# Attention into a two-layer network: one half's q sum moved to GpSimd, the w_in load gated one step later, a shorter run of fillers

## The chip, the cores and the metric

The kernel runs on one core of a Trainium2 chip. A core has five engines that run their own instruction streams in order and wait for each other by semaphores: TensorE (PE, matmuls; its weight loads are listed apart as PEld), VectorE (DVE), ScalarE (ACT), GpSimd (POOL) and SyncE (SP). Transfers between device memory and on-chip memory run on sixteen DMA engines; an engine only issues them. The metric is device time in microseconds (us) of one execution, lower is better.

## The reference

Inputs are q, k and v of shape 8 x 8 x 576 x 64 (batch, heads, positions, head width), and two matrices, w_in (512 x 2048) and w_out (2048 x 512). Per batch and head there are two attentions whose results are added:

```python
q_d = q.reshape(B, H, Sd, 4, D).mean(axis=3)      # and k_d, v_d: groups of four positions
out_up = np.repeat(sm_attn(q_d, k_d, v_d), 4, axis=2)
mask = np.abs(pos[:, None] - pos[None, :]) < 4      # a band of seven positions
out_local = softmax(masked scores) @ v
x = (out_up + out_local) -> (4608, 512)
h = x @ w_in;  out = (h / (1 + exp(-1.702 h))) @ w_out
```

The coarse branch needs sums of q, k and v over groups of four positions; the local branch needs only a band of the scores.

## The kernel before

**Stages.** The 4608 rows of x are worked on in nine groups of 512 tokens (`for g in range(n_groups)`, L1018). In group g, `mm1` (L821) computes x @ w_in in sixteen chunks of 128 columns (ffc), each of four accumulating 128x512 matmuls in `hps_mm` (L803), then the activation on ACT (`silu`, L816); `mm2` (L847) multiplies with w_out. Between these matmuls the steps of the next batch's attention are put in at numbered places: `POS_0` (L914) for group 0, `POS` for the others. Batch 0 has its own attention, written out line by line at L922 to L1016, ahead of all of this.

**Halves.** Heads are handled in two halves (qd 0 and 1) of four heads. For each half `prep_1` (L308) transposes k or q on DVE; `reduce_qk` (L327) sums q or k over groups of four in one DVE instruction (L331); `pool_qk` (L336) does the same in two GpSimd additions (L343, L347), and is used for the later batches. `bars0` and `scores0` (L409, L419) put a band mask and batch 0's local scores in PSUM (L411, L423); `scores_d` (L459) computes the coarse scores from the sums (L466); `exp0` and `exp_down` (L482, L502) take the exponentials on ACT (L485, L503).

**Values.** `load_vb0` (L258) loads batch 0's v in five chunks (i = 0 to 4) of 128, the last of 120, positions, converted to bf16. `prep_vd_pe` (L372) sums v over groups of four by matmuls with a selection matrix (L388): output part 0 reads chunks 0 and 1, part 1 chunks 1, 2 and 3, part 2 chunks 3 and 4; then a cast (L396) puts it in `vd`. `av_local0` (L513) applies the local weights to the chunks (matmuls at L516), `av_down0` (L523) the coarse ones to all three parts of `vd` (L529). `normalise0` (L543) divides on DVE (L546, L547). This runs for four head pairs hp = 0 to 3; their accumulators `o[hp]` are three PSUM tiles in turn, so hp 3 reuses the tile of hp 0 and starts once that has been normalised. `turned` (L999) transposes the results back by matmuls (L567) and copies them to `xT`, and `part` (L994) starts group 0's first w_in matmuls (L806).

**The loads' order.** All loads with conversion are issued by GpSimd, in the order of the code, and move on one software queue: k and q of batch 0, the five value chunks, then a gate, then w_in in three pieces (512, 512 and 1024 columns, L282), k and q of batch 1 (L218), two of the four pieces of w_out (L291), and in group 0's code the ten half chunks of batch 1's v (`load_vb`, L247, instructions at L249), two more pieces of w_out, and batch 2. The gate at L934 is a copy of one element out of value chunk 1 on GpSimd: as the engine works in order, nothing behind it is issued before that chunk has landed. Eight semaphores (99 to 106 in the trace) go round the software loads in turn, and a load is issued only when the load eight places ahead of it has landed.

**Who reads them.** Group 0's w_in matmuls read the first piece for ffc 0 to 3, the second for 4 to 7, the third for 8 to 15. Group 0's `mm2` takes its first eight matmuls (L884) from w_out piece 0, the next eight from piece 1, matmuls 17 to 32 from the same two pieces, and 33 to 48 from piece 2. Batch 1's v is first read by `prep_vd_pe(1, ...)` at place `VDP_0` = 36 (L915, L1055), the last half chunks by its last four matmuls.

**Fillers.** `warm` (L770) and the loop at L950 are matmuls on zeros whose results nobody reads: twelve of 512 columns, five of 128, five of 392, and four of 512 (L942, L943, L950, L964).

Of the kernel before, what the change touches and what calls it, by code (L numbers as in the profile page):

```python
# [15 lines left out]
TG = 512  # L16
# [3 lines left out]
def kernel(  # L20
# [9 lines left out]
    nc = tc.nc  # L30
# [3 lines left out]
    NQ = H // 4  # L34
# [28 lines left out]
    vbs = [persist.tile([128, 5, H, 65], BF16, name=f"vb{i}") for i in range(2)]  # L63
# [4 lines left out]
    for _ in range(2):  # L68
        t = work.tile([128, 2 * (S + SD)], FP32, name="l", tag="l", bufs=2).bitcast(BF16)
# [5 lines left out]
    PM = [psum.tile([128, 512], FP32, name=f"pm{i}") for i in range(2)]  # L75
# [3 lines left out]
    def pm_tile():  # L79
        turn["m"] += 1  # L80
        return PM[turn["m"] % 2]
# [17 lines left out]
    gate = consts.tile([1, 1], BF16, name="gate")  # L99
# [13 lines left out]
    def iota_band():  # L113
        for par in range(2):
            nc.gpsimd.iota(dm[halves[par]], pattern=[[-1, 60]], base=-4 * par,
                           channel_multiplier=1, **it)
# [97 lines left out]
    def load_1(name, src, store, b, qd):  # L214
        t = ldp.tile(
            [128, 1152], BF16, name=f"{name}b{qd}", tag=f"{name}b{qd}", bufs=2
        )
        nc.gpsimd.dma_start(  # L218
            out=t,
            in_=bass.AP(  # L220
                tensor=src.tensor, offset=src[b, 4 * qd].offset,
                ap=[[1152, 128], [1, 1152]],
            ),
        )
        store[b, qd] = t

    def load_qk(b, qd):
        load_1("k", k, kf, b, qd)
        load_1("q", q, qf, b, qd)
# [51 lines left out]
    def load_w_in(c, n):  # L281
        nc.gpsimd.dma_start(  # L282
            out=w_in_bf[:, :, c : c + n],
            in_=bass.AP(
                tensor=moe_w_in.tensor, offset=moe_w_in.offset + c,
                ap=[[d_ff, 128], [128 * d_ff, n_dmc], [1, n]],
            ),
        )

    def load_w_out(c):  # L290
        nc.gpsimd.dma_start(  # L291
            out=w_out_bf[:, 4 * c : 4 * c + 4, :],
            in_=bass.AP(
                tensor=moe_w_out.tensor, offset=moe_w_out.offset + c * 512 * d_model,
                ap=[[d_model, 128], [128 * d_model, 4], [1, d_model]],
            ),
        )
# [4 lines left out]
    def new_T(name, qd):  # L302
        n = S + 8 if name == "k" else S
        return work.tile([128, n, 2], BF16, name=f"{name}T{qd}", tag=f"{name}T{qd}", bufs=1)
# [3 lines left out]
    def prep_1(name, b, qd):  # L308
        store, dst = {"k": (kf, kT), "q": (qf, qT)}[name]
        tt = kT0[qd] if name == "k" and b == 0 else new_T(name, qd)  # L310
        t32 = tt[:, 0:S, :].rearrange("p t a -> p (t a)").bitcast(FP32)
        nc.vector.transpose(  # L312
            out=t32.rearrange("p (i c) -> p c i", c=18),
            in_=store[b, qd].bitcast(FP32).rearrange("p (c d) -> p c d", c=18),
        )
        dst[b, qd] = tt
# [5 lines left out]
    def new_qdT(b, qd):  # L322
        t = work.tile([128, SD, 2], BF16, name=f"qdT{qd}", tag=f"qdT{qd}", bufs=1)
        qdT[b, qd] = t
        return t

    def reduce_qk(b, qd, name):  # L327
        t = kdT[qd][:, 0:SD, :] if name == "k" else new_qdT(b, qd)
        src = (kT if name == "k" else qT)[b, qd]
        with nc.allow_low_precision("the sum is rounded once, as the pairwise one is"):  # L330
            nc.vector.tensor_reduce(  # L331
                out=t, in_=src[:, 0:S, :].rearrange("p (j f) a -> p j a f", f=4),
                axis=mybir.AxisListType.X, op=ALU.add,
            )

    def pool_qk(b, qd, names="kq"):  # L336
        for name, src in (("k", kT), ("q", qT)):
            if name not in names:
                continue
            sv = src[b, qd][:, 0:S, :].rearrange("p (j f) a -> p j f a", f=4)  # L340
            t1 = work.tile([128, SD * 4], FP32, name="pq", tag="pq")
            t1 = t1.rearrange("p (j f a) -> p j f a", f=2, a=2)
            nc.gpsimd.tensor_tensor(  # L343
                out=t1, in0=sv[:, :, 0:2, :], in1=sv[:, :, 2:4, :], op=ALU.add
            )
            dst = kdT[qd][:, 0:SD, :] if name == "k" else new_qdT(b, qd)
            nc.gpsimd.tensor_tensor(  # L347
                out=dst, in0=t1[:, :, 0, :], in1=t1[:, :, 1, :], op=ALU.add
            )
# [19 lines left out]
    def flat(p):  # L369
        return p.rearrange("p x n -> p (x n)")  # L370

    def prep_vd_pe(b, pv, kcs=range(3), eng=None, between=None):  # L372
        vb, vd = vbs[b], vds[b]

        def heads(x, j):
            if b == 0:
                return x.rearrange("p (hp j) d -> p hp j d", j=2)[:, :, j]
            return x.rearrange("p (m u j) d -> p m u j d", m=2, u=2)[:, :, j]

        for kc, iis in ((0, (0, 1)), (1, (1, 2, 3)), (2, (3, 4))):  # L380
            if kc not in kcs:
                continue
            c0 = 256 * (kc - kcs[0])
            for i in iis:
                if between:
                    between(kc, i)
                for j in range(2):
                    nc.tensor.matmul(  # L388
                        pv[64 * j : 64 * j + 64, c0 : c0 + D * HP],
                        lhsT=psel[b][i // 4][:, PSEL_AT[i, kc] : PSEL_AT[i, kc] + 64],  # L390
                        rhs=heads(vb[:, i, :, 0:D], j),
                        start=(i == iis[0]), stop=(i == iis[-1]),
                        tile_position=(0, 64 * j),
                    )
        cp = eng.tensor_copy if eng else nc.scalar.copy
        cp(  # L396
            out=vd[:, kcs[0] : kcs[-1] + 1, :, 0:D],
            in_=pv[:, 0 : 256 * len(kcs)].rearrange(
                "p (k h d) -> p k h d", k=len(kcs), h=HP
            ),  # L400
        )
# [111 lines left out]
    def av_local0(hp, o, chunks):  # L513
        for i in chunks:
            for j in range(2):
                nc.tensor.matmul(  # L516
                    o[:, j, 65 * i : 65 * i + 65],
                    lhsT=ez[hp // 2][:, hp % 2, j, i, :],
                    rhs=vbs[0][:, i, 2 * hp + j, :],
                    start=True, stop=True,  # L520
                )
# [248 lines left out]
    def warm(n, cols=512, t=None):  # L770
        t = pm_tile() if t is None else t
        for _ in range(n):
            nc.tensor.matmul(
                t[:, 0:cols], lhsT=wz[:, 0:128], rhs=wz[:, 0:cols], start=True, stop=True
            )
# [25 lines left out]
        return first + [lambda: avx(b, (0, 1)), lambda: avx(b, (2, 3))]  # L801

    def hps_mm(g, ffc, dmc, acc):  # L803
        n = TG // 2 if g == 1 and dmc and ffc < 9 else TG
        for c in range(0, TG, n):
            nc.tensor.matmul(  # L806
                acc[:, c : c + n],
                lhsT=w_in_bf[:, dmc, ffc * 128 : (ffc + 1) * 128],
                rhs=xT[dmc][:, g * TG + c : g * TG + c + n],
                start=(dmc == 0), stop=(dmc == n_dmc - 1 and c + n == TG),  # L810
            )
# [105 lines left out]
    o, y, x = {}, {}, {}  # L917
# [13 lines left out]
    for i in range(5):  # L931
        load_vb0(i)
    iota_band()
    nc.gpsimd.tensor_copy(out=gate, in_=vbs[0][0:1, 1, 0, 0:1])  # L934
    load_w_in(0, 512)
    load_w_in(512, 512)
    load_w_in(1024, 1024)
    for qd in range(NQ):
        load_qk(1, qd)
    load_w_out(0)  # L940
    load_w_out(1)
    warm(12)  # L942
    warm(5, 128)  # L943
    make_up()
    make_psel0()
    prep_1("k", 0, 0)
    prep_1("q", 0, 0)
    bars0(1, range(4))
    bars0(4, range(4))
    for _ in range(5):  # L950
        nc.tensor.matmul(
            PM[1][:, Q0:TG], lhsT=wz[:, 0:128], rhs=wz[:, Q0:TG],
            start=False, stop=True, skip_group_check=True,
        )
    for i in (4, 0, 1, 2, 3):
        scores0(0, i)
    exp0(0)
    reduce_qk(0, 0, "k")
    prep_1("k", 0, 1)
    reduce_qk(0, 0, "q")  # L960
    prep_1("q", 0, 1)
    reduce_qk(0, 1, "k")
    reduce_qk(0, 1, "q")
    warm(4, t=PM[0])  # L964
    bars0(4, range(4))
    bars0(1, (2, 3))
    exp_down(0, scores_d(0, 0, PB[2]))
# [6 lines left out]
    for hp in range(4):  # L974
        o[hp] = PB[hp % 3]
        y[hp] = y_tiles0()
    prep_vd_pe(
        0, PM[0], (0, 1), eng=nc.vector,
        between=lambda kc, i: av_local0(0, o[0], range(3 * ((kc, i) == (1, 3)))),
    )  # L980
    prep_vd_pe(0, PM[1], (2,), eng=nc.vector)
    exp_down(1, scores_d(0, 1, PB[2]))
    nc.scalar.preload_act_table_set("silu_and_others")
    for hp in range(4):
        av_local0(hp, o[hp], range(0 if hp else 3, 5))
        av_down0(hp, o[hp])
        normalise0(o[hp], y[hp])
    make_dm()
# [29 lines left out]
    for g in range(n_groups):  # L1018
        b = g + 1
# [69 lines left out]
```

## Time and profile before

| what | value |
|---|---|
| median of three runs | 313.85 us (313.32 to 314.01) |
| the profiled execution: its own time | 312.69 us |
| its span, first to last instruction | 310.9 us |
| granted TensorE clock in it | 1.00 |
| TensorE busy | 299.7 us, 96% |
| ACT, DVE, GpSimd busy | 203.4, 148.3, 146.9 us |
| moved by the DMA engines | 39.93 MB, 128 GB/s on average |

The span leaves out 1.8 us of the execution's own time. A profile lists instructions by line, engine, operation and operands (out<-in), with the time of one and the idle time of the engine ahead of it; the chain that ended last follows the end back through whatever released each piece of work. The time from issuing a transfer to its landing stands in the list of issues.

### The profile page before, as it was taken

Reading aid. Unit: us, or ns where it says so; the run is one execution under the profiler, and the core shown is the slowest. Engines: PE = TensorE matmul, PEld = TensorE weight load, DVE = VectorE, ACT = ScalarE, POOL = GpSimd, SP = SyncE. Lnnn points to the kernel's source line nnn. Section 1 sums busy time; section 2 is a strip of 40 time slices with the busy share of each in tenths; the row PEclk is TensorE's granted clock in tenths of the full one; section 3 lists DMA queues with packets and bytes.
Section 4 is the critical chain, followed back from the end, with each engine's and each line's share of the span. In section 5 each row is a group of like instructions: output and inputs, shape, how many; then the busy total and the mean of one; then the engine's idle time right before and its main releaser. Section 6 shows DMA issues by size and latency. Waiting matters only on the chain.

```text
span 310.9 us, 9597 instructions
## 1 busy us (share of the span) xinstructions
PE 299.7 (96%) x4138; PEld 156.2 (50%) x4181; DVE 148.3 (48%) x304; ACT 203.4 (65%) x327; POOL 146.9 (47%) x169
## 2 busy tenths in 40 slices
PE   8899999999999999999999999999999999999995
PEld 3464555665544464455545554555455544444444
DVE  6984936851694159505970499038902760000000
ACT  4755766777858786768866885589558857216511
POOL 8542393394229933894369634983396110000000
PEclk9999999999999999999999999999999999999999
DMA  6999999899527942795159705981430110010011
GB/s 110 138 208 209 185 136 216 241 201 226 161 94 163 206 120 87 166 224 139 70 168 201 177 36 174 193 211 39 137 89 34 39 70 0 34 67 36 0 67 67
DMA packets 64042, 39.93 MB, mean 128 GB/s; under 512 B 44544, under 2 KB 54912, under 8 KB 64000
## 3 DMA queue, kind: packets, MB, share of 16 engines
q0 software_dynamic: 18784, 14.94, 32.9%
q1 hardware_dynamic: 45072, 24.32, 28.0%
q8 instruction: 32, 0.52, 0.7%
q14 instruction: 10, 0.08, 0.1%
q10 hardware_dynamic: 144, 0.07, 0.1%
HBM read 44.81 MB, written 9.44 MB: 174 GB/s over the span
## 4 chain that ended last, share of the span: by engine, by line
PE 91%; DMA 2%; issue 2%; POOL 2%; ACT 1%; DVE 1%; POOLq 0%; DVEq 0%; ACTq 0%
PE pm L884 36%; PE pm L806 24%; PE pa L806 16%; PE pa L439 3%; DMA vb<-in_v_dram 2%; PE pa L884 2%; PE pa L696 2%; PE pa L674 2%; PE pa L466 2%; PE pm L899 1%; POOL vb L260 1%; PE pa L609 1%; PE pa L567 1%; PE pa L597 0%; POOL kb L218 0%
## 5 line engine op out<-in xcount | busy, mean ns | idle before, releaser
L884 PE MATMUL pm<-w_out_bf,gT 128*128 128x512 bf16 x503 | 114.6, 379 | 3.4 <-issue 3.2
L806 PEld LDWEIGHTS <-w_in_bf 128*128 128x128 bf16 x603 | 58.3, 98 | 63.8 <-issue 0.3
L806 PE MATMUL pm<-xT,w_in_bf 128*128 128x512 bf16 (+1 forms) x342 | 86.9, 375 | 0.6
L884 PEld LDWEIGHTS <-gT 128*128 128x128 bf16 x560 | 52.7, 98 | 62.4 <-issue 0.6
L817 ACT ACTIVATE gT<-pm 128x512 bf16<-128x512 f32 x88 | 52.7, 603 | 41.0 <-PE pm L806 41.0
L806 PE MATMUL pa<-xT,w_in_bf 128*128 128x512 bf16 (+1 forms) x245 | 59.0, 361 | 0.3
L511 DVE TENSOR_TENSOR es<-es,mask 128x600 bf16<-128x600 bf16 x28 | 17.2, 651 | 85.6 <-ACT es L477 85.5
L869 ACT ACTIVATE osb<-pm 128x512 f32<-128x512 f32 (+2 forms) x35 | 20.3, 583 | 30.5 <-PE pm L884 25.1
L817 ACT ACTIVATE gT<-pa 128x512 bf16<-128x512 f32 x56 | 32.1, 608 | 6.3 <-PE pa L806 6.3
L766 POOL TENSOR_TENSOR xT<-xT,od 128x576 bf16<-128x576 bf16 x12 | 15.4, 1280 | 40.0 <-DVE xT L750 40.0
L750 DVE TENSOR_TENSOR xT<-n,l 128x285 bf16<-128x285 f32 (+1 forms) x96 | 28.1, 366 | 0.0
L343 POOL TENSOR_TENSOR pq<-kT 128x576 f32<-128x576 bf16 x11 | 12.8, 1160 | 30.4 <-DVE kT L312 30.4
L871 DVE TENSOR_SCALAR osb<-pm 128x128 f32<-128x128 f32 x1 | 0.3, 291 | 53.8 <-ACT osb L869 53.8
L360 POOL TENSOR_TENSOR pq<-v 112x512 f32<-112x512 f32 x18 | 23.7, 1317 | 3.9 <-DMA v<-in_v_dram 3.9
L312 DVE STREAM_TRANSPOSE kT<-kb 128x576 f32<-128x576 f32 x16 | 19.9, 1244 | 4.4 <-DMA kb<-in_k_dram 4.4
L312 DVE STREAM_TRANSPOSE qT<-qb 128x576 f32<-128x576 f32 x16 | 19.8, 1238 | 0.3
L503 ACT ACTIVATE ed<-pa 128x864 bf16<-128x864 f32 x16 | 14.3, 894 | 7.2 <-PE pa L466 7.2
L477 ACT ACTIVATE es<-pa 128x600 bf16<-128x600 f32 x28 | 17.2, 669 | 0.1
L745 ACT ACTIVATE l<-l 128x1440 f32<-128x1440 f32 x12 | 16.8, 1404 | 0.4
L740 DVE COPY n<-pa 128x492 f32<-128x492 f32 x24 | 15.0, 665 | 2.7 <-ACT l L739 2.0
L739 ACT ACTIVATE l<-pa 128x492 f32<-128x492 f32 x24 | 12.6, 578 | 4.6 <-PE pa L696 3.7
L439 PE MATMUL pa<-qT,kT 32*64 32x60 bf16 x1120 | 15.4, 195 | 0.0
(132 smaller groups left out, 355.0 us busy)
## 6 DMA issues: line engine op xcount, KB each, us to landing
out_dram<-osb SPq DMA_DIRECT2D x34, 256.0 KB, 2.2
vf<-in_v_dram SPq DMA_DIRECT2D x60, 128.0 KB, 4.9
v<-in_v_dram SPq DMA_DIRECT2D x72, 96.0 KB, 3.1
kb<-in_k_dram POOLq DMA_DIRECT2D x16, 288.0 KB, 6.5
qb<-in_q_dram POOLq DMA_DIRECT2D x16, 288.0 KB, 8.6
w_out_bf<-in_moe_w_out_dram POOLq DMA_DIRECT2D x4, 512.0 KB, 13.2
w_in_bf<-in_moe_w_in_dram POOLq DMA_DIRECT2D x2, 512.0 KB, 6.8
w_in_bf<-in_moe_w_in_dram POOLq DMA_DIRECT2D x1, 1024.0 KB, 12.2
```

What stands on the lines that cost most here:

```text
L312: nc.vector.transpose(out=t32.rearrange("p (i c) -> p c i", c=18), in_=store[b, qd].bitcast(FP32).rearrange("p (c d) -> p c d", c=18),)
L360: eng.tensor_tensor(out=t1[0:112], in0=x[:, :, 0:2, :], in1=x[:, :, 2:4, :], op=ALU.add)
L439: nc.tensor.matmul(P[1 + r // 2][64 * par : 64 * par + 64, r % 2, 60 * i : 60 * i + 60], lhsT=kT[b, qd][rows, k0 : k0 + 64, a], rhs=qT[b, ...
L477: nc.scalar.activation(out=es[2 * qd + u][:, :, 0:300], in_=sp[u][:, :, 0:300], func=AF.Exp, scale=inv_sqrt_d,)
L511: nc.vector.tensor_tensor(out=ev, in0=ev, in1=mask, op=ALU.mult)
L745: nc.scalar.activation(out=l, in_=l, func=AF.Exp, scale=-1.0)
L750: nc.vector.tensor_tensor(out=out, in0=sub(n, *part), in1=sub(l, *part), op=ALU.mult)
L766: eng.tensor_tensor(out=xs, in0=xs, in1=sub(od[:, u, :], 0, (1, SD), (0, 4)), op=ALU.add)
L806: nc.tensor.matmul(acc[:, c : c + n], lhsT=w_in_bf[:, dmc, ffc * 128 : (ffc + 1) * 128], rhs=xT[dmc][:, g * TG + c : g * TG + c + n], star ...
L817: nc.scalar.activation(out=gT[:, ffc, :], in_=acc, func=AF.Silu, scale=GELU_SCALE)
L869: eng.activation(out=osb, in_=ap, func=AF.Copy, scale=1.0 / GELU_SCALE)
L884: nc.tensor.matmul(ops[t], lhsT=gT[:, ffc, t * 128 : (t + 1) * 128], rhs=w_out_bf[:, ffc, :], start=(ffc == 0), stop=(ffc == n_ffc - 1),)
```

## The change

GpSimd now forms the coarse sums of q of half 0 of batch 0 (`pool_qk(0, 0, "q")`) in the place of DVE's `reduce_qk(0, 0, "q")`. The gate copies from value chunk 3 instead of chunk 1, and stands, with the loads behind it, after that sum in GpSimd's order. Ten filler matmuls are dropped: the five of 128 columns, one of the five at L950, and the four of L964. DVE's two sums of half 1 follow their transposes directly. On TensorE, all of part 0 and 1 of `prep_vd_pe`, then the local products of hp 0 for chunks 0 to 3, then the coarse scores of half 1 come ahead of part 2 (which needs chunk 4); after it come the rest of hp 0's local products and all of hp 1's, ahead of hp 0's coarse ones. In group 1, ffc 9 to 12 are now also computed in two half-width matmuls for three of the four accumulation steps, as ffc 0 to 8 already were: twelve more matmuls.

```diff
     def hps_mm(g, ffc, dmc, acc):
-        n = TG // 2 if g == 1 and dmc and ffc < 9 else TG
+        n = TG // 2 if g == 1 and dmc and ffc < 13 else TG
...
     iota_band()
-    nc.gpsimd.tensor_copy(out=gate, in_=vbs[0][0:1, 1, 0, 0:1])
-    load_w_in(0, 512)
...
-    warm(12)
-    warm(5, 128)
+    warm(12)
     make_up()
...
-    for _ in range(5):
+    for _ in range(4):
         nc.tensor.matmul(
...
     exp0(0)
     reduce_qk(0, 0, "k")
+    pool_qk(0, 0, "q")
+    nc.gpsimd.tensor_copy(out=gate, in_=vbs[0][0:1, 3, 0, 0:1])
+    load_w_in(0, 512)
...
     prep_1("k", 0, 1)
-    reduce_qk(0, 0, "q")
+    reduce_qk(0, 1, "k")
     prep_1("q", 0, 1)
-    reduce_qk(0, 1, "k")
     reduce_qk(0, 1, "q")
-    warm(4, t=PM[0])
...
-    prep_vd_pe(
-        0, PM[0], (0, 1), eng=nc.vector,
-        between=lambda kc, i: av_local0(0, o[0], range(3 * ((kc, i) == (1, 3)))),
-    )
-    prep_vd_pe(0, PM[1], (2,), eng=nc.vector)
+    prep_vd_pe(0, PM[0], (0, 1), eng=nc.vector)
+    av_local0(0, o[0], range(4))
     exp_down(1, scores_d(0, 1, PB[2]))
     nc.scalar.preload_act_table_set("silu_and_others")
+    prep_vd_pe(0, PM[1], (2,), eng=nc.vector)
+    av_local0(0, o[0], range(4, 5))
+    av_local0(1, o[1], range(5))
     for hp in range(4):
-        av_local0(hp, o[hp], range(0 if hp else 3, 5))
+        if hp > 1:
+            av_local0(hp, o[hp], range(5))
         av_down0(hp, o[hp])
         normalise0(o[hp], y[hp])
```

More of the change, by code (lines that the diff above doesn't have):

```diff
@@ L370, in flat, with prep_vd_pe @@
         return p.rearrange("p x n -> p (x n)")
-    def prep_vd_pe(b, pv, kcs=range(3), eng=None, between=None):
+    def prep_vd_pe(b, pv, kcs=range(3), eng=None):
         vb, vd = vbs[b], vds[b]
@@ L384, in prep_vd_pe @@
             for i in iis:
-                if between:
-                    between(kc, i)
                 for j in range(2):
@@ L933 @@
     iota_band()
-    nc.gpsimd.tensor_copy(out=gate, in_=vbs[0][0:1, 1, 0, 0:1])
-    load_w_in(0, 512)
[L936 to L941, printed above, removed]
     warm(12)
-    warm(5, 128)
     make_up()
@@ L958 @@
     reduce_qk(0, 0, "k")
+    pool_qk(0, 0, "q")
+    nc.gpsimd.tensor_copy(out=gate, in_=vbs[0][0:1, 3, 0, 0:1])
+    load_w_in(0, 512)
+    load_w_in(512, 512)
+    load_w_in(1024, 1024)
+    for qd in range(NQ):
+        load_qk(1, qd)
+    load_w_out(0)
+    load_w_out(1)
     prep_1("k", 0, 1)
-    reduce_qk(0, 0, "q")
+    reduce_qk(0, 1, "k")
     prep_1("q", 0, 1)
-    reduce_qk(0, 1, "k")
     reduce_qk(0, 1, "q")
-    warm(4, t=PM[0])
     bars0(4, range(4))
```

## The prediction

> **What bounds the kernel.** I read the page's busy shares first, then the chain that ended last in order of time, then the timelines of GpSimd and TensorE and the DMA issues around the places that the change touches.
>
> ```profile
> PE 299.7 (96%) x4138; PEld 156.2 (50%) x4181; DVE 148.3 (48%) x304; ACT 203.4 (65%) x327; POOL 146.9 (47%) x169
> ...
> PE 91%; DMA 2%; issue 2%; POOL 2%; ACT 1%; DVE 1%; POOLq 0%; DVEq 0%; ACTq 0%
> ```
>
> TensorE is busy 96% of the span and 91% of the last chain. The rest of the chain is the beginning; its pieces are start, length, what:
>
> ```profile
> 6.32 1.73 POOL vb L260 x2
> 8.05 7.71 DMA vb<-in_v_dram
> 16.11 0.51 PE pa L466 x24
> 17.53 1.10 DVE y L547
> 18.68 0.47 PE pa L516 x10
> ```
>
> So the end hangs on value chunk 4 (issued at 8.05, landed at 15.76), then on matmuls, DVE's first normalisation (17.25 to 18.62), hp 3, and TensorE without a pause worth naming. What the change can save lies ahead of 18.7 us; what it can cost lies wherever a later load is then missed. GpSimd's timeline shows the loads (start, length, what, idle before):
>
> ```profile
> 9.00 0.47 POOL L115 IOTA dm<- 64x60 f32 x2
> 12.56 0.18 POOL L934 COPY gate<-vb 1x1 bf16<-1x1 bf16 x1 [3.08 <-DMA vb<-in_v_dram]
> 12.79 2.29 POOL L282 DMA_DIRECT2D w_in_bf<-in_moe_w_in_dram  x3
> ...
> 37.77 2.10 POOL L249 DMA_DIRECT2D vb<-in_v_dram  x3 [2.15 <-DMA w_out_bf<-in_moe_w_out_dram]
> 39.86 1.52 POOL L291 DMA_DIRECT2D w_out_bf<-in_moe_w_out_dram  x2
> ```
>
> The reader should see that the last three half chunks of batch 1's v, 25 us behind the gate, still wait for the queue: they are issued 0.28 us after w_out piece 1 lands (37.49). The stretch table gives 199 to 219 GB/s from 16 to 36 us without a hole. **The software queue is saturated from the first w_in packet to about 40 us, so a later start of w_in moves every landing behind it by as much.**
>
> **DVE and GpSimd.** Gone from DVE is one sum at 10.29, 1.29 us long. But the second half's k sum (1.29 us) moves into its place, so q's transpose still ends near 12.75 and the second scores still start at 12.79; only half 1's last sum ends earlier, near 14.0 instead of 15.14. GpSimd gets two additions of 1.147 and 0.666 us (rows L343 and L347 of later batches). It is free at 9.47 and has waited until 12.56, so they end at 9.5 + 1.15 + 0.67 = 11.3, where DVE's sum ended at 11.58: the first coarse scores (11.64) gain 0 to 0.2 us and then wait for the transpose anyway. Price 0. If GpSimd were slowed by DVE beside it, its cover lasts until the gate's chunk lands, more than 3 us.
>
> **Fillers.** TensorE idles between the first and the second scores (0.30 us at 10.56, 0.57 at 12.22). Ten fillers less (five of 128 columns and one of 392, 0.2 to 0.5 us in all, and four of 512 at 8.89, 1.04 us) make it idle longer before the same data. Price 0. As for the twenty instructions (a weight load and a matmul each) by which the stream is shorter, the trace shows one 16 KB code transfer in this stretch, from 14.28 to 15.74, ending with chunk 4's last semaphore step at 15.76. Moving it could bring chunk 4 between 0 and 0.5 us earlier (the other fetches mostly take 0.9 to 1.1 instead of 1.47), and delay it as much if it collides otherwise; the next step shows why I take 0.
>
> **The order on TensorE.** Rows of before:
>
> ```profile
> 14.55 0.35 PE L516 MATMUL pa<-vb,l 128*128 128x65 bf16 x6
> 14.86 0.42 PE L388 MATMUL pm<-vb,psel 128*64 128x256 bf16 x4
> 15.81 0.30 PE L388 MATMUL pm<-vb,psel 128*64 128x256 bf16 x2 [0.53 <-DMA vb<-in_v_dram]
> 16.04 0.58 PE L466 MATMUL pa<-qdT,kdT 32*64 32x144 bf16 x24
> ```
>
> Afterwards the path starts from chunk 3, not chunk 4. Chunks 0 to 3 landed at 11.35, 12.51, 13.52, 14.82: steps of 1.16, 1.01, 1.30. Without w_in's descriptors written beside the fourth (12.79 on), I take 1.08, the mean of the first two: 14.6, with 14.5 and 14.82 as ends. From there: two matmuls of L388 (0.22), eight of L516 (0.41 by the six in 0.31), 24 of L466 (0.51), four of L388 (0.42), some 0.1 for two switches of shape: 14.64 + 1.66 = 16.3, where part 2's cast began at 16.22. Chunk 4 is there by then, even at 15.76. So TensorE's idle 0.53 us is filled, but the cast starts within -0.05 to +0.3 us of where it did, most likely +0.1. The first normalisation follows 1.03 us later as before, and hp 1's local products, now done early, leave TensorE idle in front of hp 3, which waits for that normalisation. **Expected gain at the start: none, -0.1 us.**
>
> **The gate.** It opened 0.28 us after its chunk (12.51 to 12.79). With chunk 3 at 14.6 w_in is issued at 14.88, 2.1 us later. Not all of that is lost, because w_in could not run at once:
>
> ```profile
> GB/s 152 160 155 149 152 152 157 155 155 157 157 152 152 149 138 131 122 90 73 61 45 46 210 97 87 42 10 0 0 31 20 72 123 143 164 205 195 215 205 174
> ```
>
> These are 40 slices of 12 to 16 us. The value chunks fade out by 14.3; the first w_in packet starts at 14.32, and full rate is reached at 15.3. By 16.0 some 171 packets of 1 KB had gone; at 197 per us that equals a start at full rate at 15.13. For an issue into an empty queue the nearest row is the first load of the kernel, k at 1.24: first packet 1.40 us after issue, and its bytes by 4.0 us (196 KB at 190 per us) equal full rate from 2.97, 1.73 after issue. w_in's descriptors take 0.80 us against 0.69, so 1.8: 14.88 + 1.8 = 16.68. **The queue moves by 16.68 - 15.13 = 1.55 us.** Ends: chunk 3 at 14.5 and 1.3 us to full rate (the shortest first packet of the later k loads is 1.27) give 0.95; 14.82 and 2.0 give 2.0.
>
> By the Trainium skill (DMA: Bandwidth & Descriptors, Specifications), a GpSimd-issued transfer has a first-byte latency of about 1 us; an estimate by that is a queue moved by 0.75 us. The rows here show 1.27 to 1.49 for k and 1.53 for w_in, so the trace speaks for the dearer price, and the sum does not use the page.
>
> **Who misses it.** Landing now, plus 1.55, against the reader (landing from the issue list: issue plus time to landing):
> - w_in pieces: 18.75, 21.29, 26.56, read at 20.89, 25.05, 29.37: still 0.6 us or more in time. k and q of batch 1 shift DVE's sums from 37.6 to 39.2, read at 40.31: in time.
> - w_out piece 1: 37.49 to 39.04, read by the ninth L884 matmul at 39.36: just in time.
> - batch 1's v, last half: 43.00 to 44.55; its reader is the 13th of the fourteen L388 matmuls, at 44.02. TensorE's queue took its release 0.10 us after landing, and some 0.15 goes to the start: late by 0.78.
> - w_out piece 2 (39.86 + 7.2 = 47.0) to 48.57, read by the 33rd L884 matmul at 47.83: with 0.15 late by 0.9, the first 0.78 of which is already lost.
>
> ```profile
> 43.43 0.97 PE L388 MATMUL pa<-vb,psel 128*64 128x256 bf16 x14
> 44.34 1.04 PE L884 MATMUL pa<-w_out_bf,gT 128*128 128x512 bf16 x4
> ...
> 47.83 0.38 PE L884 MATMUL pm<-w_out_bf,gT 128*128 128x512 bf16 x1
> ```
>
> Both readers have about 0.7 us to spare, so TensorE loses the shift less 0.7: 0.85 us, and any gain or loss at the start of up to that size is swallowed there. Behind it TensorE has no idle time that could give it back.
>
> **Group 1's halves.** Eight half-width matmuls run from 59.65 to 60.53, 0.110 us each, two of them 0.220 against 0.216 for a full one: twelve pairs cost 0.05 us. The shift of the later stream by two pairs I price at 0 (loops repeat in 32.35 to 32.42 us).
>
> **Sum.** 0 + 0 + 0.85 + 0.05, the start swallowed: +0.9 us on the profiled execution's 312.69 (span 310.9 and 1.8 around it). That execution is 1.16 below the median of the runs, so I add it to the median: 314.75.
>
> **Rivals.**
> - *The spare time swallows it.* If the queue moves by 0.9 to 1.3 us, the readers miss 0.2 to 0.6 us at most: 313.7 to 314.4, within 0.2% (0.63 us, about what this kernel's measurement can tell from no change). For it: the low ends above. Against it: k's slow first packets.
> - *The values come earlier, so it is faster.* One mechanism: w_in's descriptor writing is what slows the value chunks, in the slices from 13.3 on where the rate falls from 152 to 45. If chunk 3 lands at 14.2 or before, the cast starts at 15.9 and the first normalisation 0.4 us earlier or more; the gate then opens at 14.5 and with a short start the queue moves by about 0.7, which the spare time covers. At 14.0 this gives 0.65 us: 313.2. It decides from chunk 3 before 14.3. Against it: chunks 1 and 2, undisturbed, came in steps of 1.0 to 1.16, which puts chunk 3 at 14.5.
> - *TensorE loses its full rate.* The first eleven fillers start 427 ns apart, the later ones up to twice as fast, so TensorE starts at half rate. The four dropped fillers were 1.04 of 2.88 us busy from 9 to 13. If it fell back, the 3 to 5 us of matmuls behind 12.8 would cost 1.5 to 2.5 us more: 316. Against it: the 0.57 and 0.53 us pauses of before did not trigger it. The Trainium skill (TensorE: Matmul & The Clock Gate, Part 1) has the half rate return after an idle window of about 3.4 us; no pause here is that long.
> - *The edits do not reach the path* (GpSimd's sum and the code fetch, above): then the gate alone decides, as forecast.
>
> **Chances.** Forecast, later loads: 0.55, own range 314.5 to 315.6. Swallowed: 0.28. Faster: 0.12. Half rate: 0.05. Slower 0.60, same 0.28, faster 0.12. The range, 313.5 to 315.8, leaves out most of the faster case and the half rate.
>
> **What would show it.** The gate copy near 14.7 and w_in at 14.9; first w_in packet near 16.3; w_in's first piece landing at 20.3, batch 1's last values near 44.5; a pause of about 0.8 us in the L388 group at 44 or in front of the 33rd L884 matmul near 48.5; the first normalisation between 17.2 and 17.6. It is wrong if w_in's landing moves by under 1 us, or if TensorE shows no pause between 43 and 49 us.

## The result and the profile after

The changed kernel takes **316.26 us** (median of 8 runs, 315.26 to 317.43) against 313.93 us for the kernel before in the same rounds (8 runs, 313.07 to 315.44). The ratio is **1.0072**, 95% interval 1.0047 to 1.0097: slower by some 2.3 us, where 0.9 was forecast. The profiled execution took 315.53 us, with a span of 313.8 us (before: 310.9).

The page of the changed kernel: the busy times, the 40 slices of the granted clock, and the shares of the chain that ended last.

```profile
span 313.8 us, 9646 instructions
...
PE 304.2 (97%) x4183; PEld 157.3 (50%) x4183; DVE 149.6 (48%) x303; ACT 203.4 (65%) x327; POOL 150.4 (48%) x171
...
PEclk9989999999999999999999999999999999999999
...
PE 80%; DMA 12%; ACT 2%; DVE 2%; POOL 2%; issue 1%; DVEq 0%; POOLq 0%; ACTq 0%
```

Two things are new. DMA had 2% of the chain and has 12%. The clock row has an 8 in its third slice (15.7 to 23.5 us): part of it ran at less than full clock. TensorE's 4.5 us more of busy time (299.7 before) are not to be read as cost: the trace of before lacks 43 matmul records (4138, with 4181 weight loads).

The chain of the changed kernel in order of time (start, length, what; the first 62 us):

```profile
7.19 8.17 DMA vb<-in_v_dram
...
15.41 0.18 POOL gate L949
...
15.64 5.53 DMA w_in_bf<-in_moe_w_in_dram
...
21.45 19.42 DMA w_out_bf<-in_moe_w_out_dram
...
41.16 4.81 DMA vb<-in_v_dram
...
46.01 0.41 PE pa L386 x4
```

Read downwards: value chunk 3 lands at 15.36, the gate opens, w_in is issued at 15.64, w_out and the last half chunks of batch 1's v wait for their place in the queue, and TensorE's last sums of those values wait for their landings (45.97 on this chain, 46.38 for the last half chunk). Before, no load after the start was on the chain. (Lines of the changed code stand two lower: L386 here is L388 before, L882 is L884, L647 is L649.)

GpSimd's timeline in the changed kernel (start, length, what, idle before and its cause), then TensorE's:

```profile
10.79 0.67 POOL L347 TENSOR_TENSOR qdT<-pq 128x288 bf16<-128x288 f32 x1
15.41 0.18 POOL L949 COPY gate<-vb 1x1 bf16<-1x1 bf16 x1 [3.96 <-DMA vb<-in_v_dram]
15.64 2.31 POOL L282 DMA_DIRECT2D w_in_bf<-in_moe_w_in_dram  x3
...
41.16 2.03 POOL L249 DMA_DIRECT2D vb<-in_v_dram  x3 [2.43 <-DMA w_out_bf<-in_moe_w_out_dram]
43.16 1.53 POOL L291 DMA_DIRECT2D w_out_bf<-in_moe_w_out_dram  x2
```

```profile
44.30 1.02 PE L882 MATMUL pa<-w_out_bf,gT 128*128 128x512 bf16 x4
45.25 1.57 PE L386 MATMUL pa<-vb,psel 128*64 128x256 bf16 x14
46.76 1.04 PE L882 MATMUL pa<-w_out_bf,gT 128*128 128x512 bf16 x4
```

The fourteen L386 matmuls took 0.97 us before and take 1.57; the 0.6 between are two waits of some 0.3 us, for half chunks that land at 45.97 and, the last one, at 46.38 (43.00 before). At the end of this group TensorE is at 46.82, before it was at 44.40: 2.4 us late. In this execution 1.8 of them were there when the group began (45.25 against 43.43); they come from the start. At the end of the span it is 2.9 late.

The stretches from 14 to 19 us in the changed kernel; the last three columns are the granted clock, the DMA share and GB/s:

```profile
14.00:14.50 0.50, 0.50 (x11) 0.40 (x12) 0.42 (x1) 0.50 (x1) 0.00 (x0) 1.00 2.90 72
15.00:15.50 0.50, 0.10 (x2) 0.10 (x1) 0.00 (x0) 0.50 (x2) 0.09 (x1) 0.83 0.06 1
16.50:17.00 0.50, 0.50 (x24) 0.47 (x16) 0.13 (x1) 0.00 (x0) 0.50 (x1) 0.50 0.00 0
17.50:18.00 0.50, 0.50 (x9) 0.26 (x6) 0.08 (x1) 0.50 (x1) 0.50 (x2) 0.50 0.63 53
18.50:19.00 0.50, 0.50 (x26) 0.49 (x24) 0.00 (x0) 0.50 (x1) 0.50 (x2) 0.75 1.20 199
```

From 15 to 17 us hardly a byte moves, and full rate returns at some 18.2 (15.3 before). And the clock is at half from 15.33 to 18.75 us.

### The profile page after: what moved, and what is told of

The parts are those of the page before. It is cut to its first block, busy times and chain, and to the rows that moved or that the text cites. A ratio compares the mean times of both kernels' runs of the same rounds, so it can differ in the third digit from the quotient of the medians.

```text
span 313.8 us, 9646 instructions
## 1 busy us (share of the span) xinstructions
PE 304.2 (97%) x4183; PEld 157.3 (50%) x4183; DVE 149.6 (48%) x303; ACT 203.4 (65%) x327; POOL 150.4 (48%) x171
## 4 chain that ended last, share of the span: by engine, by line
PE 80%; DMA 12%; ACT 2%; DVE 2%; POOL 2%; issue 1%; DVEq 0%; POOLq 0%; ACTq 0%
PE pm L882 35%; PE pm L804 22%; PE pa L804 13%; DMA w_out_bf<-in_moe_w_out_dram 6%; DMA vb<-in_v_dram 4%; PE pa L437 3%; PE pa L694 2%; PE pa L672 2%; DMA w_in_bf<-in_moe_w_in_dram 2%; PE pa L464 1%; PE pm L897 1%; ACT l L640 1%; DVE xT L647 1%; ACT l L629 1%; POOL vb L260 1%
## 5 line engine op out<-in xcount | busy, mean ns | idle before, releaser
L882 PE MATMUL pm<-w_out_bf,gT 128*128 128x512 bf16 x528 | 119.4, 379 | 0.0
L804 PEld LDWEIGHTS <-w_in_bf 128*128 128x128 bf16 x615 | 59.5, 98 | 63.1 <-issue 0.7
L804 PE MATMUL pm<-xT,w_in_bf 128*128 128x512 bf16 (+1 forms) x370 | 89.0, 369 | 0.3 <-ACT osb L867 0.2
L882 PEld LDWEIGHTS <-gT 128*128 128x128 bf16 x560 | 52.8, 98 | 62.3 <-issue 0.4
L509 DVE TENSOR_TENSOR es<-es,mask 128x600 bf16<-128x600 bf16 x28 | 18.7, 707 | 82.7 <-ACT es L475 82.6
L764 POOL TENSOR_TENSOR xT<-xT,od 128x576 bf16<-128x576 bf16 x12 | 16.7, 1394 | 38.1 <-DVE xT L748 37.8
L437 PE MATMUL pa<-qT,kT 32*64 32x60 bf16 x1120 | 15.4, 195 | 0.0
```

Of the source, the lines that this page charges most:

```text
L437: nc.tensor.matmul(P[1 + r // 2][64 * par : 64 * par + 64, r % 2, 60 * i : 60 * i + 60], lhsT=kT[b, qd][rows, k0 : k0 + 64, a], rhs=qT[b, ...
L509: nc.vector.tensor_tensor(out=ev, in0=ev, in1=mask, op=ALU.mult)
L764: eng.tensor_tensor(out=xs, in0=xs, in1=sub(od[:, u, :], 0, (1, SD), (0, 4)), op=ALU.add)
L804: nc.tensor.matmul(acc[:, c : c + n], lhsT=w_in_bf[:, dmc, ffc * 128 : (ffc + 1) * 128], rhs=xT[dmc][:, g * TG + c : g * TG + c + n], star ...
L882: nc.tensor.matmul(ops[t], lhsT=gT[:, ffc, t * 128 : (t + 1) * 128], rhs=w_out_bf[:, ffc, :], start=(ffc == 0), stop=(ffc == n_ffc - 1),)
```

## The experiments

The main theory was that the gate alone (chunk 3 instead of 1, two chunks later) makes the loss, through the queue. Rivals: the new order on TensorE and the half clock at the start; the dropped fillers; GpSimd's sum. The half-width chunks of group 1, priced 0.05 us, were not run alone. The ratios are against the kernel before, run on the same chip in turn; its medians there lie between 313.09 and 314.07.

| run | ratio [95%] | w_in issued | batch 1's v all landed | first normalisation | first activation of group 1 |
|---|---|---|---|---|---|
| before | 1 | 12.79 | 43.00 | 17.25 | 61.60 |
| after | 1.0072 [1.0047, 1.0097] | 15.64 | 46.38 | 19.07 | 64.30 |
| e1: after, gate 1 | 1.0033 [1.0014, 1.0052] | 13.04 | 43.80 | 17.67 | 62.09 |
| e2: before, gate 3 | 1.0099 [1.0075, 1.0123] | 15.39 | 46.08 | 17.23 | 63.80 |
| e3: after, fillers back | 1.0112 [1.0078, 1.0145] | 16.48 | 46.99 | 18.75 | 65.61 |
| e4: before, new order | 1.0034 [1.0015, 1.0054] | 13.24 | 43.98 | 19.32 | 63.68 |
| e8: before, fewer fillers | 1.0010 [0.9995, 1.0025] | 13.05 | 43.17 | 17.40 | 62.30 |
| e12: before, GpSimd's sum | 0.9999 [0.9978, 1.0021] | 12.94 | 43.98 | 17.48 | 62.40 |

The last four columns are from one profiled execution each; chunk 3's landing alone lies between 14.7 and 16.2 us in the profiled executions of all kernels.

### One part undone, one part alone: e1 to e4

e1 is the changed kernel with the gate back, e2 the kernel before with the gate moved:

```diff
e1   -    nc.gpsimd.tensor_copy(out=gate, in_=vbs[0][0:1, 3, 0, 0:1])
e1   +    nc.gpsimd.tensor_copy(out=gate, in_=vbs[0][0:1, 1, 0, 0:1])
e2   -    nc.gpsimd.tensor_copy(out=gate, in_=vbs[0][0:1, 1, 0, 0:1])
e2   +    nc.gpsimd.tensor_copy(out=gate, in_=vbs[0][0:1, 3, 0, 0:1])
```

> The changed kernel with the gate back on value chunk 1; everything else stays changed. Queue theory (the loss is w_in's later issue, carried by the full software queue to batch 1's v at 45 us): w_in is issued near 12.8 to 13.2 us, batch 1's last value half lands near 43.0 to 43.5, and the loss of 2.3 us shrinks to what is left of the start, 0 to 0.7 us. Start theory (the loss is the new matmul order and TensorE's half rate before 19 us): the first normalisation stays near 18 to 19 us and the kernel stays 1.5 us or more slower than before.

> The kernel before with the gate on value chunk 3 and nothing else. Queue theory: w_in is issued 2.3 to 2.9 us later, batch 1's last value half lands that much later (45.3 to 45.9), the time rises by that less some 0.6 us: 1.7 to 2.3 us slower. Start theory: within 0.3 us of before.

Measured: 1.0033 and 1.0099. The gate alone costs 3.1 us, all that the whole change costs and more (1.7 to 2.3 were expected); with the gate back, 1.0 us stays, somewhat above the 0.7 allowed for. TensorE of e2:

```profile
37.59 1.90 PE L884 MATMUL pm<-w_out_bf,gT 128*128 128x512 bf16 x8
40.48 1.02 PE L884 MATMUL pm<-w_out_bf,gT 128*128 128x512 bf16 x4 [0.99 <-DMA w_out_bf<-in_moe_w_out_dram]
...
44.75 0.91 PE L388 MATMUL pa<-vb,psel 128*64 128x256 bf16 x12
46.21 0.30 PE L388 MATMUL pa<-vb,psel 128*64 128x256 bf16 x2 [0.55 <-DMA vb<-in_v_dram]
```

The second wait is the one of the changed kernel, at the same place (there it lies inside the group), with the old order, all fillers and a full clock. The first one the changed kernel does not have: with TensorE on time, the ninth L884 matmul already waits 0.99 us for w_out piece 1, which lands at 40.44 (37.49 before). In the changed kernel's profile TensorE came 1.8 us later, and that piece (40.87) was there. **The gate is the cause of the main loss.**

e3 is the changed kernel with its ten fillers back, e4 the kernel before with the new order on TensorE:

```diff
e3   +    warm(5, 128)
e3   -    for _ in range(4):
e3   +    for _ in range(5):
e3   +    warm(4, t=PM[0])
e4   -    prep_vd_pe(0, PM[0], (0, 1), eng=nc.vector, between=...)
e4   -    prep_vd_pe(0, PM[1], (2,), eng=nc.vector)
e4   +    prep_vd_pe(0, PM[0], (0, 1), eng=nc.vector)
e4   +    av_local0(0, o[0], range(4))
     ...
e4   +    prep_vd_pe(0, PM[1], (2,), eng=nc.vector)
e4   +    av_local0(0, o[0], range(4, 5))
e4   +    av_local0(1, o[1], range(5))
     ...
```

> The changed kernel with the ten fillers put back. Queue theory: TensorE keeps its full rate and the first normalisation comes near 17.5 to 18 instead of 19.07, but batch 1's v still lands near 46, so the time stays 2.0 us or more above before. Start theory: 1 to 1.8 us of the 2.3 come back.

> The kernel before with the new order of the first value products alone (part 0 and 1, local products of hp 0 for chunks 0 to 3, coarse scores, part 2, the rest). Queue theory: the first normalisation moves by -0.1 to +0.4 us and the time by as much. Start theory, as far as it blames the order: 0.5 to 1 us slower.

Measured: 1.0112 and 1.0034. The fillers do not bring the time back; by the medians e3 is no faster than the changed kernel (316.16 against 316.26). Its first normalisation came at 18.75, not at 17.5 to 18; chunk 3 landed late in that execution (16.19). The order alone costs 0.34%, with the old gate, some 1.1 us, which is what the start theory gave; the first normalisation moves by 2.07 us, where the main theory had 0.4 at most. TensorE of e4:

```profile
15.76 0.30 PE L388 MATMUL pm<-vb,psel 128*64 128x256 bf16 x2 [1.07 <-DMA vb<-in_v_dram]
15.99 0.57 PE L516 MATMUL pa<-vb,l 128*128 128x65 bf16 x8
16.49 0.93 PE L466 MATMUL pa<-qdT,kdT 32*64 32x144 bf16 x24
```

Chunk 3 landed at 15.71 in this execution, and the local products that filled this wait before now stand behind it. From 16.10 to 19.51 the clock is at half: the 24 coarse scores take 0.93 us, as in the changed kernel, where e1 with a full clock shows 0.58:

```profile
15.32 0.42 PE L514 MATMUL pa<-vb,l 128*128 128x65 bf16 x8
15.67 0.58 PE L464 MATMUL pa<-qdT,kdT 32*64 32x144 bf16 x24
16.18 0.49 PE L386 MATMUL pm<-vb,psel 128*64 128x256 bf16 x4
```

The half clock is not there in every execution. Six of ten of e1 have a mean clock below 0.996; they take 314.78 us on average, the four others 313.50. The kernel before averages 313.26 beside them, so most of what e1 loses is the half clock. In e4 the two below take 314.96 and the four others 313.63: about half of its loss. (3.41 us at half clock take 0.005 off the mean of an execution.)

### The dose: e5, e6, e7

The kernel before with the gate on chunk 0 (e5), 2 (e6) and 4 (e7) instead of 1.

> The kernel before with the gate on value chunk 0, nothing else: w_in issued 1.1 us earlier. Queue theory: batch 1's last value half lands about 1.1 us earlier, but it was in time already, so the time stays (within 0.4 us), unless w_in now slows the value chunks, which would show as chunk 4 landing later and the first normalisation after 17.3. Start theory says nothing of it.

> The kernel before with the gate on value chunk 2: w_in issued 1.0 us later. Queue theory with the whole shift of the issue passed on and 0.7 us to spare at batch 1's v: 0.3 to 0.6 us slower. If instead a part of the shift is hidden by the value chunks' own drain, as the prediction had it: no change.

> The kernel before with the gate on value chunk 4: w_in issued 3.2 to 3.5 us later. Queue theory: 0.8 to 1.0 us slower than with chunk 3, so 3.5 to 4 us above before; the pause in front of batch 1's v grows by as much and w_out piece 1 or the first w_in piece may be missed too.

| gate on chunk | w_in issued | w_in's first step landed | batch 1's v all landed | ratio [95%] |
|---|---|---|---|---|
| 0 | 11.94 | 17.01 | 42.71 | 1.0015 [0.9987, 1.0042] |
| 1 (before) | 12.79 | 17.80 | 43.00 | 1 |
| 2 | 13.83 | 18.80 | 43.91 | 1.0033 [1.0017, 1.0050] |
| 3 (e2) | 15.39 | 20.22 | 46.08 | 1.0099 [1.0075, 1.0123] |
| 4 | 16.28 | 21.20 | 47.20 | 1.0123 [1.0099, 1.0147] |

Issue and landing move together, within 0.25 us, and the time follows from chunk 2 on. From w_in's issue to its first packet it takes 1.50 to 1.53 us with gates 1 to 4 and 1.66 with gate 0, whether chunks still drain ahead of it or the queue is empty. **Of a later issue 0.2 us at most was hidden by the values ahead of it** (e2: issued 2.60 us later, first step landed 2.42 later). An earlier one (e5) gains nothing that can be measured.

Who waits changes with the dose. e6 cost 1.0 us where 0.3 to 0.6 was expected, and in its profile TensorE waits for no late load. In e7 the pause in front of batch 1's v was expected to grow, and it is gone: TensorE loses the time earlier, to w_in's first piece, and the L388 group then takes 0.98 us. TensorE of e7:

```profile
22.88 1.03 PE L806 MATMUL pm<-xT,w_in_bf 128*128 128x512 bf16 x2 [1.59 <-DMA w_in_bf<-in_moe_w_in_dram]
...
46.66 0.98 PE L388 MATMUL pa<-vb,psel 128*64 128x256 bf16 x14
```

### Fewer fillers, and GpSimd's sum: e8, e12

e8 is the kernel before without the ten fillers. e12 is it with `pool_qk(0, 0, "q")` on GpSimd, the gate and the loads behind it, and DVE's order of the changed kernel.

> The kernel before without the ten fillers, nothing else. Queue theory: nothing moves in the queue; no change, except in executions in which TensorE falls to half rate for a window before 19 us, which cost about 1 to 1.5 us each. If the fillers hold the rate, such executions appear here and the median rises by 0.3 to 1 us; if the order's empty wait alone causes them, none appear.

> The kernel before with the first q half's sum on GpSimd (and DVE's order as in the change), nothing else; the gate stays on chunk 1. By the prediction's step: the sum ends near 11.4, the second scores still start near 12.8 to 13.1, and the time is the same within 0.3 us.

Measured: 1.0010 and 0.9999. Neither edit can be told from no change by itself. But five of the ten executions of e8 have a mean clock below 0.996, which only one of 92 of the kernel before has: without these fillers the clock is lost in part of the executions, with the old order too. It costs nothing there: the five take 313.79 us on average, the five others 313.84. The profiled execution of e8 is one with a full clock, so where its half clock lies is not shown.

### A shorter queue: e9 and its control e10

w_in's third piece is loaded with 512 columns instead of 1024, so 512 KB less lie ahead of batch 1; e9 does it in the changed kernel, e10 in the kernel before. The last 512 columns of w_in are left out, and ffc 12 to 15 compute with the weights of 8 to 11, so the product is another one while the work stays.

```diff
-                lhsT=w_in_bf[:, dmc, ffc * 128 : (ffc + 1) * 128],
+                lhsT=w_in_bf[:, dmc, (ffc - ffc // 12 * 4) * 128 : (ffc - ffc // 12 * 4 + 1) * 128],
...
-    load_w_in(1024, 1024)
+    load_w_in(1024, 512)
```

> The changed kernel, but only the first 512 of the last 1024 columns of w_in are loaded, and chunks 12 to 15 compute with the weights of 8 to 11 (so a part of the product is another one; the work of every engine stays). Gate, order and fillers stay changed. Queue theory: 512 KB less ahead of batch 1's loads give back about 2.5 us of queue, its v lands near 43.5 again, and the time falls from 2.3 to 3 us above before to 0.3 to 1.2, what the start costs. Start theory: the time stays where it was.

> The control: the same shortened w_in load in the kernel before (chunks 12 to 15 compute with the weights of 8 to 11). Queue theory: every later landing 2.5 us earlier, but nothing waited for them: within 0.3 us of before, at most 0.3 us faster where executions had batch 1's loads late.

Measured: e9 1.0018 [0.9992, 1.0044], e10 0.9981 [0.9960, 1.0002]. In e9 w_in is issued as late as in the changed kernel (15.52), yet batch 1's v has landed at 43.96 and the group has no wait:

```profile
45.69 0.97 PE L386 MATMUL pa<-vb,psel 128*64 128x256 bf16 x14
```

So the late issue does no harm by itself; it costs because the queue has no slack up to batch 1's values. In e9 the half clock shows again: five executions below 0.996 take 314.86 us on average, the five above 313.41. (The profiled one has it, so its group starts late; but 43.96 would be in time for the kernel before too, and w_out piece 1 landed at 38.83.)

### A second place, GpSimd's wait for w_out: e11, e13, e14

The trace shows a second reader that the late queue delays, one that the prediction did not look at. GpSimd waits in its order for w_out's piece 3 (the gate of batch 2's values), and only then adds `od` to `xT`. Before, this addition ended (50.91) just ahead of DVE's next product; in the changed kernel it runs beside it. GpSimd, then DVE, of the changed kernel:

```profile
52.53 0.17 POOL L918 CAST vf<-w_out_bf 1x1 f32<-1x1 bf16 x1 [2.81 <-DMA w_out_bf<-in_moe_w_out_dram]
52.68 1.20 POOL L658 TENSOR_TENSOR xT<-xT,od 128x576 bf16<-128x576 bf16 x1
```

```profile
50.35 0.31 DVE L647 TENSOR_TENSOR od<-n,l 128x144 f32<-128x144 f32 x1 [0.55 <-ACT l L640]
53.46 0.59 DVE L647 TENSOR_TENSOR od<-n,l 128x144 f32<-128x144 f32 x1 [0.81 <-ACT l L640]
```

The same product takes 0.31 us alone and 0.59 beside the addition. This is not peculiar to a late queue: in the profiles of e8 and e12, with w_in as early as before and no loss that can be told, it takes 0.84 and 0.88; in that of e6 0.89. To test it, the gate of batch 2's values is moved to piece 2, in the kernel before (e11), in the changed kernel (e13) and in e1 (e14):

```diff
-            load_v(2, gate=after(w_out_bf[0:1, 12, 0:1], nc.gpsimd))
+            load_v(2, gate=after(w_out_bf[0:1, 8, 0:1], nc.gpsimd))
```

> The kernel before with batch 2's first value load held back by w_out's piece 2 instead of piece 3, so that GpSimd is free for its additions of x some 2.5 us earlier (near 47 instead of 49.6). If the second place of loss is GpSimd's addition running beside DVE's product at 51 us, this product takes 0.31 us in every execution and the time is the same or up to 0.5 us less than before; if that place does not matter, or the earlier value load disturbs w_out's last piece, the same or slower.

> The changed kernel with one wait of GpSimd's moved: batch 2's values are issued once w_out's piece 2 has landed instead of piece 3, so GpSimd no longer stands at L918 until 52.5 us and its xT addition (1.20 us) can end before DVE's product od at 53.5 us. Theory A, the late queue costs in two places (batch 1's last values in front of TensorE, then GpSimd's wait for w_out): od takes 0.31 us again instead of 0.59, and the ratio falls from 1.0072 by 0.1 to 0.2 points, to 1.0052 to 1.0062. Theory B, only the wait for batch 1's values costs: od is 0.31 us all the same, but the ratio stays at 1.0072 within its interval, since another wait ends last. Theory C, the loads issued earlier push other loads back: the ratio rises above 1.0085.

> The changed kernel with the gate of w_in back at value chunk 1 (1.0033 by itself) and the same move of GpSimd's wait to w_out's piece 2. Theory A, part of those 0.33% comes from GpSimd's wait and DVE's product beside its addition: 1.0015 to 1.0025. Theory B, the 0.33% come from the start alone (values' order on TensorE, its half rate from about 15 us in part of the executions): 1.0033 within its interval.

Measured: e11 0.9991 [0.9969, 1.0012], e13 1.0081 [1.0053, 1.0110], e14 1.0010 [0.9991, 1.0030]. In e13 the product is back at 0.31 us and group 1's first activation comes at 64.04 instead of 64.30. But the time is no better than the changed kernel's. DVE, GpSimd and TensorE of e13 show where the 0.26 us went:

```profile
53.47 0.31 DVE L647 TENSOR_TENSOR od<-n,l 128x144 f32<-128x144 f32 x1 [0.81 <-ACT l L640]
```

```profile
78.55 1.41 POOL L360 TENSOR_TENSOR pq<-v 112x512 f32<-112x512 f32 x1 [5.25 <-DMA vf<-in_v_dram]
```

```profile
82.84 0.26 PE L672 MATMUL pa<-ed,vd 48*64 48x144 bf16 x4 [0.46 <-POOL vd L363]
```

Batch 2's values, now issued from 50.47 on, before w_out's last piece has landed (52.87), come later at their end: their second copies need 7.8 us from issue to landing (median) instead of 6.1. GpSimd starts summing them at 78.55 instead of 77.92, and TensorE waits 0.46 us for that sum, where it did not wait in the changed kernel. The expectation that the ratio falls by 0.1 to 0.2 points failed, though its step (the product at 0.31) came true. For e14 the ratio is 0.23 points under e1's, but the intervals overlap; it isn't settled. Its executions split as e1's do: seven below 0.996 take 314.87 us, the five others 313.93.

No version tried is clearly faster than the kernel before.

## Why the prediction was right in its direction and wrong in its size

**The chain was right.** Later gate, later queue, batch 1's last half chunk late, TensorE waits in the L388 group, nothing gives it back. The gate alone (e2) does that, the profile of the changed kernel has the pause at the place named (0.6 us instead of 0.8, with TensorE already 1.8 us late), and the shortened queue (e9) removes it.

**The step that failed is the size: "The queue moves by 16.68 - 15.13 = 1.55 us."** Measured: w_in's issue moved by 2.85 us, the first step of its landing by 2.83 (17.80 to 20.63), batch 1's last landing by 3.38. The 1.28 us between 1.55 and 2.83 are two errors.
- *"Not all of that is lost, because w_in could not run at once"* took 0.55 us off. I had read the slow start of w_in as a wait for the value chunks to drain. The dose runs show 1.50 to 1.53 us to the first packet behind any gate from 1 to 4, so the delay moves with the issue. My comparison row, k's first load, is another load and reaches full rate sooner: 1.73 us after its issue by my reckoning, where w_in took 15.13 - 12.79 = 2.34.
- *Chunk 3 at 14.6* was 0.76 us early: it landed at 15.36. Of this, 0.48 was there at chunk 2 (14.00, before 13.52). Chunk 2 landed between 13.52 and 14.39 in the profiled executions of all kernels, so the single profile that I built on was the earliest of them: bad luck. The other 0.28 is the step, 1.36 instead of 1.08. I had reckoned that without w_in's descriptors beside it the fourth chunk would come in a step like the first two. Without them the step was 1.14 to 1.80 us (six profiles), with them 1.18 to 1.80 (ten), so the descriptors do not show as what slows it. It was in the trace of before that it came 1.30 behind chunk 2; I explained that away.

With 3.38 for the last half chunk the same sum gives 2.4 us, near the 2.3 measured: its matmul, the 13th of the group, starts at 44.13 before (I had 44.02), and in the changed kernel it starts 0.14 after the landing, so 44.13 - 43.00 - 0.14 = 0.99 us were to spare, and 3.38 - 0.99 = 2.39. That it fits so well is partly luck. For the gate alone the sum comes out low: 2.1 against 3.1 us (e2), nothing against 1.0 (e6), 3.2 against 3.9 (e7). What adds 0.7 to 1.0 us there is open. The rest of the shift in the queue, 3.38 against 2.83, came on the way; its cause I did not test.

**The readers.** w_in's pieces and k and q of batch 1 were in time, as forecast. w_out piece 2 was not late on TensorE, since the loss had already been taken. w_out piece 1, which the forecast had just in time, is late as soon as the queue moves by the measured amount and TensorE does not: e2 waits 0.99 us for it, the larger of its two waits. That GpSimd itself stands in front of w_out piece 3 was missing in the list; the cost of that in the changed kernel stays unproven, as e13 gave 0.26 us back and lost 0.46 elsewhere.

**DVE and GpSimd, priced 0.** GpSimd's sum ended at 11.46 (forecast 11.3). The second scores came at 13.09 instead of 12.79, so not quite free in that execution, but e12 alone shows no cost (0.9999). **Fillers, priced 0:** e8 agrees in the time (1.0010, not told from 1), but not in the clock, which falls in half of its executions.

**The order on TensorE, priced -0.1.** Wrong: e4 costs 0.34%. The first normalisation came at 19.07, 1.8 us late, not within 0.3. TensorE of the changed kernel:

```profile
13.09 0.23 PE L421 MATMUL pm<-qT,kT 32*128 32x120 bf16 x2 [1.01 <-DVE qT L312]
...
15.40 0.43 PE L386 MATMUL pm<-vb,psel 128*64 128x256 bf16 x2 [0.56 <-DMA vb<-in_v_dram]
15.76 0.62 PE L514 MATMUL pa<-vb,l 128*128 128x65 bf16 x8
16.31 0.93 PE L464 MATMUL pa<-qdT,kdT 32*64 32x144 bf16 x24
17.17 0.64 PE L386 MATMUL pm<-vb,psel 128*64 128x256 bf16 x4
```

The path waits for chunk 3, and everything behind it runs at half clock. The rival *TensorE loses its full rate*, which had a chance of 0.05, thus came true in this execution: 1.05, 0.30, 1.01 and 0.56 us of pauses between 9 and 15.4, then 3.41 us at half clock. But it isn't what made the time: the late values at 46 us are waited for whether TensorE gets there 1.3 us earlier or not. In the changed kernel the executions with full clock (317.43, 316.38, 316.15) are not faster than the others (315.26 to 316.55). As the prediction said of the start, up to the size of the wait behind it a loss is swallowed there; with the gate on chunk 1 (e1, e4, e14) or the queue shortened (e9) the half clock shows, as 0.9 to 1.5 us between the two kinds of execution. In e8 it does not show, and why is open.

What the prediction drew from the Trainium skill (TensorE: Matmul & The Clock Gate, Part 1) misled there: by its idle window of about 3.4 us, pauses of at most 1.05 us should leave the rate alone. The measurement decides: the rate fell behind them. The length of the half rate, 3.41 us or twice that, does agree with the page's window. The same page tells (A second HAM failure mode) of a kernel whose many short idles made the rate swing, which is nearer to this trace.

**Still open:** which executions lose the clock. Leaving the fillers out brings it (e8, 5 of 10), and the new order with all fillers does in 2 of 6 (e4); but e1 has it in some executions and not in others, with one code, and e3 shows a pause of 1.14 us and a full clock. Open too is why the gate alone (1.0099) and the changed kernel with its fillers back (1.0112) come out higher than the change itself (1.0072), with intervals that touch.

## What to carry to other kernels

Where a load queue is full without a hole for tens of microseconds, whatever stands in front of its first load moves the far end by its whole delay: follow the queue to every load that somebody waits for, and move the delay there undiminished unless a row shows the same load starting sooner. A gate should open on the earliest landing that serves it, and a step of a sequence that the trace shows to be longer should be taken as it stands, not explained away. One profile gives a landing only within its scatter (0.9 us for chunk 2 here). A loss at the start and a late load behind it did not add up here (1.0 and 3.1 us apart, 2.3 together), so test each with the other removed.

## What the runs showed of the hardware

- **The half clock after short pauses.** Granted clock at half for 3.41 us (changed kernel, e4) or 6.83 us (e9, e13, e14), where the longest TensorE pause ahead of it, from 7 us on, was 1.05 to 1.07 us. In e7, 3.41 us at half clock follow a pause of 1.59 us at 21.3, the wait for w_in. The profiles of e1, e3 and e8 have pauses of 1.05 to 1.14 us there and no half clock. A mean clock below 0.996 came in 5 of 8 executions of the changed kernel, 6 of 10 of e1 and 5 of 10 of e8 (only the fillers left out), and in 1 of 92 of the kernel before in the rounds of e1 to e14.
- **The first packet of a software load** comes 1.50 to 1.53 us after w_in's issue behind gates 1 to 4, with other loads draining or none, and 1.66 behind gate 0.
- **DVE's product and GpSimd's addition take turns.** The product `od` takes 0.31 us alone; beside the addition it took 0.38 (e1), 0.40 (e2), 0.59 (after), 0.65 (e7), 0.84 (e8), 0.88 (e12), 0.89 (e6) and 1.29 (e3), and in all eight it ended 0.17 us after the addition did. By these ends it does not run slower, it stands until the other is done. The Trainium skill (SBUF — State Buffer, SBUF: two separate sides) states just that: a DVE instruction with two operands in on-chip memory and a GpSimd instruction that reads there exclude each other for a whole instruction. The trace agrees.
